# Attention and gated feed-forward on one core: side lists and sessions of score blocks, casting loads for chunks 1 and 2, and weights loaded behind chunk 0

## The chip, the cores and the metric

The kernel runs on one NeuronCore of a Trainium2 chip. The metric is the device time of one execution in microseconds, from the first to the last instruction. Five instruction streams run beside one another: TensorE (PE, with its weight loads as PEld), VectorE (DVE), ScalarE (ACT), GpSimd (POOL) and SyncE (SP); each works through its own instructions in the order in which they are written. Loads and stores are issued from the streams of SP, ACT and POOL; a load that also converts its type is issued from POOL.

## The reference

Four batches, eight heads, 768 positions, 64 numbers per head. Heads 0, 2 and 6 ("retrieval") see all earlier positions; the five others ("stream") see the first 4 positions and the last 64. The attention output, 3072 rows of 512, goes through two matrices with a gate between them.

```python
scores = scale * np.matmul(q, k.transpose(0, 1, 3, 2))
stream_keep = causal & (is_sink | in_win)              # n_sink = 4, window = 64
mask = np.where(retr, causal, stream_keep)             # by head
a = np.exp(np.where(mask, scores, -1e9) - max)
a = a / (np.sum(a, axis=-1, keepdims=True) + 1e-09)
x = np.matmul(a, v)                                    # then (3072, 512)
h = x @ w_in                                           # 512 -> 2048
g = h * (1.0 / (1.0 + np.exp(-beta * h)))
out = g @ w_out                                        # 2048 -> 512
```

All inputs and the output are float32; the kernel's matmuls take bfloat16.

## The kernel before

**Chunks.** The work is cut into 8 chunks, a batch and a half of the sequence each (384 positions, three tiles of 128). Before, the order alternates two batches: (0, first half), (1, first half), (0, second half), (1, second half), then the same for batches 2 and 3. A first half has 6 score blocks of 128x128 for a retrieval head and 5 for a stream head; a second half has 15 and 6.

**Stages of a chunk.** Keys and queries come in, are brought to bfloat16 and transposed, so that a pair of heads fills the 128 rows of KT and QT, 64 rows each. `attention(c, p)` (L561) works on one pair of heads: scores on TensorE (L603; the two heads sit on the two halves of the array's rows and run side by side), exponentials on ScalarE (L615), masks multiplied on VectorE (L630 to L648), the products with the values on TensorE (L663), whose 65th column gives the row sum, then the reciprocal and the scaling on VectorE (L667, L671). `x_transposed` (L674) transposes the result on TensorE (L683) or by DMA (L688). `first_part` (L695) multiplies by w_in: 16 groups of 4 matmuls (L701), each into a PSUM bank; ScalarE takes tanh of it (L703), VectorE combines both to the gate gT (L705) and frees the bank. `second_part` (L708) multiplies gT by w_out: three rows of 16 matmuls (L719) in steps of four, then the copy out of PSUM (L730, L732) and the store (L735).

**PSUM.** Eight banks: four for scores (`S_BANKS`), four for everything else (`G_BANKS`). A score group takes two rounds of banks for two heads, so up to four banks, and holds up to 384 columns in each; for the first two chunks it takes one round.

**Masks of the first chunks.** For chunks 0 and 1 the masks are added on TensorE: an identity matmul writes 0 or a large negative number into the bank ahead of the scores (L590).

**Loads.** For chunks 0, 1 and 2 keys and queries are loaded as float32 by SP and ACT, a pair of heads at a time (L379), cast on VectorE or ScalarE (L440) and transposed on TensorE (L448), three 128x128 pieces for each of k and q of a pair. From chunk 3 on POOL issues casting loads of rows (L417) and SP transposes them by DMA (L462). Values are loaded as float32 by SP (L392) and cast by POOL or VectorE (L497). The weights w_in and w_out come as four casting loads each from POOL (L399, L405); each is held back by a one-element copy (`held`, L365) until some earlier load has landed, by the table `W_AFTER`: w_in's first quarter behind the first values of chunk 0, the second behind chunk 1's last queries, the next two behind chunk 1's values, w_out behind w_in.

**What sets the order.** All streams are scheduled by hand, by a planner in the same file (class `Plan`): each step is a task with an engine, a cost, what it depends on and a priority; the planner runs through time, always gives the next free engine its best ready task, and the instructions are then written in that order. TensorE prefers attention; first and second products (`F1`, `F2`) fill up, by their running number and `F2_LAG`. The order is fixed when the program is built, and no engine changes it at run time. Where the plan shows TensorE idle before 36 us, matmuls on zeros are put in (`fill`, L811), and ten larger ones stand at the very start (`idle`, L338).

Of the kernel before, what the change touches and what calls it, by code (L numbers as in the profile page):

```python
# [16 lines left out]
class Slots:  # L17
# [18 lines left out]
    def take(self, n):  # L36
        order = sorted(range(len(self.free)), key=lambda i: (self.free[i], i))[:n]
        for i in order:
            self.free[i] = INF
        return order  # L40


class Hold:


    def __init__(self, slots, n=1):
        self.slots, self.n = slots, n
        slots.holds.append(self)
        self.got = None
        self.users = 0  # L50
        self.until = 0.0

    @property
    def buf(self):
        return self.slots.names[self.got[0]]

    @property
    def bufs(self):
        return [self.slots.names[i] for i in self.got]


class Task:
    __slots__ = ("name", "alts", "deps", "prio", "emit", "take", "drop", "mode", "land", "n_wait", "after",
                 "done", "start", "engine", "bias", "seq", "follow")

    def __init__(self, name, alts, deps, prio, emit, take=(), drop=(), mode=128, land=None, bias=0.0, follow=()):
        self.name, self.alts, self.prio, self.emit = name, alts, prio, emit
        self.deps = [d for d in deps if d is not None]
        self.take, self.drop, self.mode, self.land, self.bias = list(take), list(drop), mode, land, bias
# [5 lines left out]

class Plan:
# [3 lines left out]
    SWITCH = 100.0  # L80

    def __init__(self):
        self.tasks = []
        self.fill = None
# [7 lines left out]
    def run(self, pick):  # L92
        free = dict.fromkeys(self.SEM, 0.0)
        ready = {e: [] for e in self.SEM}
        for t in self.tasks:
            t.n_wait = len(t.deps) + len(t.follow)
            for d in t.deps + t.follow:
                d.after.append(t)

        def enter(t):  # L100
            for e, occ, lat in t.alts:
                at = max((d.start if e == d.engine == "PE" else d.done + self.SEM[e] for d in t.deps), default=0.0)
                at = max([at] + [d.start for d in t.follow])
                ready[e].append((at, t, occ, lat))
        for t in self.tasks:
            if not t.n_wait:
                enter(t)
        self.order = []
        self.mode = 128
        dma_free = 0.0  # L110
        lanes = {"hw": [], "sw": []}
        n = len(self.tasks)
        left = n
        while left:
            best = None
            for e, lst in ready.items():
                first = INF
                floor = free[e]
                cand = []
                for it in lst:  # L120
                    at = max(floor, it[0])
                    need = {}
                    for h in it[1].take:
                        if h.got is None:
                            need[h.slots] = need.get(h.slots, 0) + h.n
                            if not h.slots.turn(h):
                                at = INF
                    for slots, count in need.items():
                        at = max(at, slots.when(count))
                    if it[1].land is not None:  # L130
                        ln = lanes[it[1].land[0]]
                        if len(ln) >= 8:
                            at = max(at, ln[-8] + 60.0)
                    cand.append((at, it))
                    first = min(first, at)
                if first < INF and (best is None or first < best[0]):
                    best = (first, e, [c for c in cand if c[0] <= first])
            if best is None:
                self.stuck = [t for t in self.tasks if t.start is None]
                raise RuntimeError("the plan is stuck: " + ", ".join(t.name for l in ready.values() for _, t, _, _ in l[:4]))  # L140
# [3 lines left out]
            it = pick(e, now, [c[1] for c in cand])  # L144
            at, t, occ, lat = it
            for _, en in [(None, x[0]) for x in t.alts]:
                ready[en] = [x for x in ready[en] if x[1] is not t]
            if e == "PE":
                if t.mode != self.mode:
# [4 lines left out]
            if t.land is not None:  # L154
                kind, service = t.land
                begin = max(dma_free, now + occ + 1000.0)
                dma_free = begin + service
                t.done = dma_free + 1000.0
                lanes[kind].append(t.done)
            else:  # L160
                t.done = now + lat
            for h in t.take:
                if h.got is None:
                    h.got = h.slots.take(h.n)
            for h in t.drop:
                h.users -= 1
                h.until = max(h.until, t.done)
                if h.users == 0:
                    for i in h.got:
                        h.slots.free[i] = h.until + 55.0  # L170
            self.order.append(t)
            left -= 1
            for a in t.after:
                a.n_wait -= 1
                if a.n_wait == 0:
                    enter(a)
        self.end = max(t.done for t in self.tasks)
        return self.order

# [3 lines left out]
N_IDLE = 10  # L183
ROUNDS = 2
F2_LAG = 16.0
RAMP = 24000.0
RAMP_C = 2
FILL_END, FILL_SPARE = 36000.0, 120.0
N_F32 = 3
W_AFTER = [("v", 0, 0), ("q", 1, 3), ("v", 1, 0), ("v", 1, 2), ("wi", 1), ("wi", 2), ("wo", 0), ("wo", 1)]  # L190
C2_AFTER = ("wi", 2)
V2_AFTER = ("wi", 3)


def XT_PE(c, m):
    return c < 4 or (c == 7 and m % 2)
# [3 lines left out]
def kernel(  # L200
# [21 lines left out]
    stream = [h for h in range(H) if not retr[h]]  # L222
# [642 lines left out]
```

## Time and profile before

| what | value |
|---|---|
| median of 3 runs | 236.01 us (235.86 to 238.44) |
| span of the profiled execution | 236.1 us, which is also its time |
| instructions | 5174 |
| TensorE busy | 227.0 us, 96% |
| VectorE busy | 147.6 us, 63% |
| ScalarE busy | 157.3 us, 67% |
| GpSimd busy | 75.8 us, 32% |
| mean granted TensorE clock | 0.993 |
| read from HBM | 27.27 MB |

The page of the profile has the busy time of each engine, the span in 40 slices, the DMA queues, the chain of work that ended last, and the costliest groups of instructions. A group is named by its line in the kernel, engine and operation, with the tile written and the tiles read; behind the bar stand its busy time and the mean time of one, then the idle time of the engine just ahead of them and who ended it. Matmuls are pipelined: the time of one is longer than the distance from one to the next, so prices on TensorE are taken from start to start. The timeline gives start, length and instruction; what stands in brackets is the engine's idle time ahead of it and what ended that. Numbers like 64*128 are the rows and columns of the array in use.

### The profile page before, as it was taken

What the parts mean: (1) busy time and instruction counts of PE and PEld (TensorE: products, weight loads), DVE (VectorE), ACT (ScalarE), POOL (GpSimd) and SP (SyncE); (2) the same over time, 40 slices, a digit from 0 to 9 for tenths busy, and PEclk for the clock granted to TensorE, in tenths of its full rate; (3) what the DMA queues carried; (4) which work ended last, traced back from release to release, by engine and by line L of the source; (5) the groups of instructions that cost most, each with busy time, mean ns of one, the idle gap of its engine ahead of it and who ended that gap; (6) DMA issues with size and microseconds to landing.
All of it is one profiled execution on the core that took longest, in us unless ns stands there. A gap on an engine that the chain in (4) does not pass through costs nothing.

```text
span 236.1 us, 5174 instructions
## 1 busy us (share of the span) xinstructions
PE 227.0 (96%) x1898; PEld 125.8 (53%) x1898; DVE 147.6 (63%) x350; ACT 157.3 (67%) x339; POOL 75.8 (32%) x152
## 2 busy tenths in 40 slices
PE   7969989989999999999999999999999999999994
PEld 3546565544655545555554554555555555555553
DVE  5874878786857546558983886677756443434320
ACT  2947959797745569749786886889975645555400
POOL 4302431841991781799921334030000000000000
PEclk9997999999999999999999999999999999999999
DMA  6999999999899999999994696472121001111112
GB/s 199 247 212 230 174 172 261 254 176 100 158 168 186 158 199 152 122 193 229 130 174 105 148 131 117 109 149 61 21 78 47 24 22 46 47 44 44 44 47 89
DMA packets 93482, 31.10 MB, mean 132 GB/s; under 512 B 79744, under 2 KB 90512, under 8 KB 93456
## 3 DMA queue, kind: packets, MB, share of 16 engines
q1 hardware_dynamic: 56688, 22.10, 41.3%
q0 software_dynamic: 35904, 8.13, 41.0%
q10 hardware_dynamic: 864, 0.53, 0.7%
q8 instruction: 15, 0.25, 0.5%
q14 instruction: 11, 0.09, 0.1%
HBM read 27.27 MB, written 6.29 MB: 142 GB/s over the span
## 4 chain that ended last, share of the span: by engine, by line
PE 87%; DMA 5%; DVE 3%; SPq 2%; ACT 1%; issue 1%; ACTq 0%
PE bank L719 36%; PE bank L701 35%; PE bank L603 7%; PE bank L663 5%; DMA qs<-in_q_dram 5%; SPq L392 1%; PE bank L448 1%; PE bank L590 1%; PE bank L683 1%; SPq L379 1%; DVE gT L705 1%; DVE x L671 1%; ACT es L615 1%; ACT th L703 0%; DVE qkb L280 0%
## 5 line engine op out<-in xcount | busy, mean ns | idle before, releaser
L703 ACT ACTIVATE th<-bank,beta_h 128x384 f32<-128x384 f32 x128 | 74.4, 585 | 39.6 <-PE bank L701 31.7
L705 DVE SCALAR_TENSOR_TENSOR gT<-th,bank 128x384 bf16<-128x384 f32 x128 | 70.2, 551 | 46.8 <-ACT th L703 42.3
L701 PE MATMUL bank<-xT,w_in_sb 128*128 128x384 bf16 x512 | 95.9, 326 | 0.2 <-ACT xT L280 0.2
L719 PE MATMUL bank<-w_out_sb,gT 128*128 128x512 bf16 (+1 forms) x400 | 96.0, 371 | 0.0
L701 PEld LDWEIGHTS <-w_in_sb 128*128 128x128 bf16 x512 | 48.3, 98 | 37.2 <-issue 1.5
L719 PEld LDWEIGHTS <-gT 128*128 128x128 bf16 x400 | 37.0, 98 | 35.5 <-issue 2.6
L615 ACT ACTIVATE es<-bank 128x384 bf16<-128x384 f32 (+1 forms) x96 | 37.5, 477 | 11.6 <-PE bank L603 11.5
L615 ACT ACTIVATE esL<-bank 128x384 bf16<-128x384 f32 x68 | 28.0, 506 | 1.1 <-PE bank L603 1.0
L280 POOL COPY KO<-KT 128x128 bf16<-128x128 bf16 (+3 forms) x23 | 8.0, 370 | 48.5 <-DVE KO L280 17.8
L603 PE MATMUL bank<-QT,KT 64*128 64x128 bf16 (+2 forms) x258 | 22.9, 252 | 0.3 <-ACT QT L280 0.3
L417 POOL DMA_DIRECT2D qs<-in_q_dram x30 | 22.7, 786 | 0.9 <-issue 0.9
L417 POOL DMA_DIRECT2D ks<-in_k_dram x30 | 22.5, 797 | 0.0
L730 ACT ACTIVATE osb<-bank 128x512 f32<-128x512 f32 (+1 forms) x16 | 8.9, 559 | 13.3 <-DVE osb L732 9.9
L603 PEld LDWEIGHTS <-KT 64*128 64x128 bf16 x258 | 10.5, 95 | 13.3 <-issue 11.6
L671 DVE TENSOR_TENSOR x<-bank,rec 128x384 bf16<-128x384 f32 x32 | 17.3, 550 | 0.4
L630 DVE TENSOR_TENSOR es<-es,M 128x768 bf16<-128x768 bf16 (+1 forms) x24 | 12.5, 529 | 4.9 <-ACT es L615 4.9
L732 DVE TENSOR_SCALAR osb<-bank 128x512 f32<-128x512 f32 (+1 forms) x11 | 6.8, 617 | 10.3 <-PE bank L719 10.3
L667 DVE RECIPROCAL rec<-bank 128x6 f32<-128x6 f32 x32 | 6.0, 191 | 11.3 <-PE bank L663 11.2
L663 PEld LDWEIGHTS <-es 128*128 128x128 bf16 x268 | 10.6, 98 | 3.9 <-issue 0.7
L663 PE MATMUL bank<-VX,es 128*128 128x65 bf16 x200 | 11.6, 195 | 0.2 <-DVE gT L705 0.2
L280 POOL COPY VO<-VX 128x512 bf16<-128x512 bf16 (+2 forms) x7 | 6.0, 860 | 9.1 <-PE bank L603 5.3
L663 PEld LDWEIGHTS <-esL 128*128 128x128 bf16 x204 | 7.0, 97 | 1.1
(76 smaller groups left out, 149.9 us busy)
## 6 DMA issues: line engine op xcount, KB each, us to landing
vs<-in_v_dram SPq DMA_DIRECT2D x24, 256.0 KB, 5.4
out_dram<-osb SPq DMA_DIRECT2D x23, 256.0 KB, 2.2
ks<-in_k_dram SPq DMA_DIRECT2D x12, 192.0 KB, 5.9
w_in_sb<-in_moe_w_in_dram POOLq DMA_DIRECT2D x4, 512.0 KB, 8.0
w_out_sb<-in_moe_w_out_dram POOLq DMA_DIRECT2D x4, 512.0 KB, 9.0
qs<-in_q_dram SPq DMA_DIRECT2D x10, 192.0 KB, 8.6
ks<-in_k_dram POOLq DMA_DIRECT2D x30, 64.0 KB, 5.7
qs<-in_q_dram POOLq DMA_DIRECT2D x30, 64.0 KB, 4.3
```

Source lines behind the costliest of these rows:

```text
L280: (nc.scalar.copy if e == "ACT" else eng[e].tensor_copy)(out=out, in_=in_)
L417: ROW[name, c, t] = [dma(f"row{name}{c}.{t}.{a}", "POOL", 750, 850, list(deps), lambda e, t=t, a=a, r=r, i=i, src=src: e.dma_start(out=hol ...
L603: nc.tensor.matmul(to, kk(), of, start=not by_pe, stop=(r, at + n) == ends[a, r] or not by_pe)
L615: EX[a].append(P.add(f"exp{c}.{p}", [act(w * 128)], [t], prio, lambda _, a=a, place=place, w=w, bank=bank: nc.scalar.activation(out=es.buf ...
L630: masks.append(P.add(f"mask{c}.{p}", [dve(2 * (hi - lo) * 128, 0.53)], [EX[0][r], EX[1][r], t_mask], prio, lambda _, lo=lo, hi=hi: nc.vect ...
L663: nc.tensor.matmul(view()[:, i, a, 0:D + 1], es.buf[:, (base[a] + at) * 128:(base[a] + at + 1) * 128], val(), start=(j == 0), stop=(j == l ...
L671: nc.vector.tensor_mul(xo, view()[:, :, :, 0:D], rec.buf.to_broadcast([128, HT, 2, D]))
L701: nc.tensor.matmul(bank.buf[:, 0:HALF], w_in_sb[:, mo, fi * 128:(fi + 1) * 128], XTH[c].buf[:, mo, :], start=(mo == 0), stop=(mo == MO - 1))
L703: t = P.add(f"th{c}.{fi}", [act(HALF, 97)], [t, t_beta], c * 100, lambda _, fi=fi, bank=bank, th=th: nc.scalar.activation(out=th.buf, in_= ...
L705: GATE[c, fi] = P.add(f"gate{c}.{fi}", [dve(HALF)], [t], c * 100, lambda _, fi=fi, bank=bank, th=th: nc.vector.scalar_tensor_tensor(out=GH ...
L719: nc.tensor.matmul(bank.buf[:, 0:hi - lo], GH[c].buf[:, fi, ns * 128:(ns + 1) * 128], w_out_sb[:, fi, lo:hi], start=(fi == 0), stop=(fi == ...
L730: nc.scalar.activation(out=osb.buf[:, 0:h - l], in_=src, func=ACTF.Copy, scale=0.5)
```

## The change

The kernel is written anew in these points. The computation stays the same.

* **Chunk order and pairs.** Chunks now go batch by batch: (0, first half), (0, second half), (1, first half) and so on. In batch 0 heads are paired as neighbours, (0,1), (3,2), (4,5), (6,7); in the other batches as before, p with p + 4.
* **Side lists and sessions.** The score blocks of a chunk form two lists, one for the heads on each half of the array. From chunk 1 on, a session takes several banks for each side from these lists, up to four blocks (512 columns) in each, across heads. A first half is done in two sessions of 3 + 3 banks, a second half in three, with 4 + 3, 4 + 3 and 3 + 3; chunk 1 in four smaller ones. All exponentials of a chunk go into one large tile (`es_r`, two of them). Chunk 0 still goes pair by pair, and it alone adds its masks on TensorE; all others multiply them on VectorE, head by head.
* **Banks.** All eight banks are one pool.
* **Loads.** Of chunk 0, the first two pairs of k and q are loaded as float32 by SP and ACT and cast on the engines; the other half, and chunks 1 and 2 whole, come as casting loads of four heads from POOL, which need no cast. All values come as casting loads from POOL straight into VX. The weights follow in a fixed order on POOL's queue (`ORDER`): w_in's first two quarters behind chunk 0, then chunk 1's k and q, w_in's rest, chunk 1's values, w_out, chunk 2. The holding copies are gone. Chunks 3 to 7 keep row loads and DMA transposes.
* **Transposes.** Each head's 64 columns are transposed by themselves into one half of the bank's rows: six matmuls with 64 output rows for each of k and q of a pair, where three with 128 stood. x is transposed on TensorE for chunks 0 to 3 and all of chunk 7 (before: half of chunk 7).
* **Planner.** Loads are modelled as three queues that share the DMA engines (`Rings`). First and second products and the sessions from chunk 1 on stand in a written order (`P.script`, `STAGE_0`, `stage`), from which the planner may bring forward a task among the next eight. Fillers end at 16 us of the plan.

The core of the diff:

```diff
-N_F32 = 3
-W_AFTER = [("v", 0, 0), ("q", 1, 3), ("v", 1, 0), ("v", 1, 2), ("wi", 1), ("wi", 2), ("wo", 0), ("wo", 1)]
-FILL_END, FILL_SPARE = 36000.0, 120.0
+FILL_END, FILL_SPARE = 16000.0, 120.0
+STAGE_0 = [(3, 0, 0), (3, 0, 1), (3, 0, 2), (3, 0, 3), (4, 0, None)]
+SESSIONS = {0: [(3, 3), (3, 3)], 1: [(4, 3), (4, 3), (3, 3)]}
+SESSIONS_1 = [(3, 2), (3, 2), (3, 3), (2, 2)]
+ORDER = ["wi0", "wi1", "k1a", "q1a", "k1b", "q1b", "wi2", "wi3", "v10", "v11", "v12", "wo0", "wo1", "wo2", "wo3",
+         "k2a", "k2b", "q2a", "q2b", "v20", "v21", "v22"]
-    return c < 4 or (c == 7 and m % 2)
+    return c < 4 or c == 7
-    S_BANKS = Slots(banks[0:4])
-    G_BANKS = Slots(banks[4:8])
+    BANKS = Slots(banks)
-    esS = ring(4, [128, 14 * 128], BF16, "es")
-    esL = ring(2, [128, 32 * 128], BF16, "esL")
+    es_r = ring(2, [128, 75 * 128], BF16, "es")
+    def load_sw(c, h, name, prio):
+        to = Hold(qkb)
+        t = dma(f"ld{name}{c}.{h}", "POOL", 750, 768, 32, [], lambda e: e.dma_start(
+            out=to.buf.rearrange("p a t d -> p a (t d)"),
+            in_=rows_of(k if name == "k" else q, c)[h:h + 4].rearrange("a (p t) d -> p a (t d)", t=HT)), take=[to], prio=prio, follow=[t_m1])
...
+        LD["v", c, t] = dma(f"ldv{c}.{t}", "POOL", 1000, 256, 64, list(deps) + [t_ones[id(x)] for x in V_r.names], lambda e: e.dma_start(
+            out=VH[c].buf[:, t, :, 0:D], in_=rows_of(v, c)[:, t * 128:(t + 1) * 128, :].rearrange("h p d -> p h d")), take=[VH[c]], prio=prio, follow=follow)
...
-                for t in range(HT):
-                    nc.tensor.transpose(tp[:, t, :], hold.buf[:, i, t].rearrange("p a d -> p (a d)"), ident)
+                for t in range(HT):
+                    for a, (_, hold, i) in enumerate(src):
+                        nc.tensor.transpose(tp[half(a), t, :], hold.buf[:, i, t], ident)
...
+    def session(c, parts, prio, lane):
...
+        work = [(a, lo, SIDE[c, a][1][lo:lo + n], Hold(BANKS)) for a, lo, n in parts]
...
+            for _, a, h, kk, i, n, place, bank, ends in sorted(todo, key=lambda x: x[:2]):
+                nc.tensor.matmul(bank.buf[:, place * 128:(place + n) * 128], kk[1](), QH[c].buf[half(a), WHERE[c][h][1], i * 128:(i + n) * 128], start=not by_pe, stop=not by_pe or ends)
...
+            x = P.add(f"exp{c}.{a}.{lo}", [act(w * 128)], [t], prio, lambda _, e0=e0, w=w, bank=bank: nc.scalar.activation(
+                out=EH[c].buf[:, e0 * 128:(e0 + w) * 128], in_=bank.buf[:, 0:w * 128], func=ACTF.Exp, scale=scale), drop=[bank])
```

**POOL at the start** shows the loads' new order. First before, from the casts that hold the weights back (w_in_sb, w_out_sb: the weights; vs, qs: staged values and queries; KO: keys collected for stream heads; VO: values for them):

```order
L368 CAST w_in_sb<-vs_79 1x1
L399 DMA w_in_sb<-in_moe_w_in_dram 128x4x512
L280 COPY KO_87<-KT_83 128x128
L280 COPY KO_88<-KT_84 128x128 x2
L368 CAST w_in_sb<-qs_74 1x1
L399 DMA w_in_sb<-in_moe_w_in_dram 128x4x512
```

Then now, from the first load on:

```order
L490 DMA qkb_75<-in_k_dram 128x4x192
L490 DMA qkb_76<-in_q_dram 128x4x192
L497 DMA VX_97<-in_v_dram 128x8x64 x3
L502 DMA w_in_sb<-in_moe_w_in_dram 128x4x512 x2
L490 DMA qkb_77<-in_k_dram 128x4x192
L490 DMA qkb_78<-in_q_dram 128x4x192
L490 DMA qkb_79<-in_k_dram 128x4x192
L490 DMA qkb_80<-in_q_dram 128x4x192
L502 DMA w_in_sb<-in_moe_w_in_dram 128x4x512 x2
L385 COPY KO_93<-KT_89 128x128 x4
L497 DMA VX_98<-in_v_dram 128x8x64 x3
```

Two quarters of w_in now stand ahead of chunk 1's keys and queries, and nothing holds them back but their place.

**ScalarE in the middle of the program** shows what a visit to the scores leaves it to do (es, esL: exponentials; th: tanh of a first product). Before:

```order
L615 ACTIVATE esL_101<-bank_64 128x384
L615 ACTIVATE esL_101<-bank_65 128x384
L615 ACTIVATE esL_101<-bank_66 128x384
L615 ACTIVATE esL_101<-bank_63 128x384
L703 ACTIVATE th_113<-bank_68,beta_h 128x384
L615 ACTIVATE esL_101<-bank_64 128x384
L615 ACTIVATE esL_101<-bank_65 128x384
```

And now:

```order
L698 ACTIVATE es_104<-bank_70 128x512
L698 ACTIVATE es_104<-bank_67 128x512
L698 ACTIVATE es_104<-bank_65 128x512
L698 ACTIVATE es_104<-bank_68 128x512
L698 ACTIVATE es_104<-bank_66 128x512
L698 ACTIVATE es_104<-bank_69 128x512
L698 ACTIVATE es_104<-bank_64 128x512
L787 ACTIVATE th_114<-bank_70,beta_h 128x384
```

Four banks of 384 columns per visit have become seven of 512, and the first tanh behind them reuses the bank that the first of these exponentials read.

**TensorE's mode changes**, counted over its whole order: scores stand in 52 separate stretches before and in 25 now.

## Prediction before the change was run

> **What bounds the kernel now.** I read the head of the page first, then two long windows (columns after the stretch: its length, busy us of PE, PEld, DVE, ACT and POOL with their instruction counts, the granted clock, the DMA share and GB/s).
>
> ```profile
> span 236.1 us, 5174 instructions
> PE 227.0 (96%) x1898; PEld 125.8 (53%) x1898; DVE 147.6 (63%) x350; ACT 157.3 (67%) x339; POOL 75.8 (32%) x152
> PE 87%; DMA 5%; DVE 3%; SPq 2%; ACT 1%; issue 1%; ACTq 0%
> ...
> 0.00:34.00 34.00, 29.06 (x309) 17.37 (x310) 24.33 (x73) 22.66 (x56) 10.95 (x37) 0.95 1.00 206
> 34.00:236.00 202.00, 197.89 (x1591) 108.46 (x1589) 123.28 (x277) 134.65 (x284) 64.83 (x116) 1.00 0.81 119
> ```
>
> TensorE is the bound: 87% of the last-ended chain. The kernel has two parts. After 34 us PE is busy 197.9 of 202 us; 3.2 of the rest lie behind the last matmul, so that part ends sooner only if PE has less to do in it. Before 34 us the clock averages 0.95 and there are holes. So I ask two questions: when does PE become dense, and what is left for it then?
>
> In the PE timeline before is dense from 33.66 us on (start, length, instruction):
>
> ```profile
> 23.66 0.82 PE L701 MATMUL bank<-xT,w_in_sb 128*128 128x384 bf16 x4
> ...
> 33.66 7.96 PE L701 MATMUL bank<-xT,w_in_sb 128*128 128x384 bf16 x48
> ...
> 222.33 10.56 PE L719 MATMUL bank<-w_out_sb,gT 128*128 128x512 bf16 x64
> ```
>
> From 33.66 to the end it needs 236.1 − 33.7 = 202.4 us. The last product ends at 222.33 + 10.56 = 232.9, hence the 3.2 us tail, which the change leaves alone.
>
> **Prices of PE work**, from start to start in the dense part:
>
> ```profile
> 195.73 0.81 PE L701 MATMUL bank<-xT,w_in_sb 128*128 128x384 bf16 x4
> 196.38 1.03 PE L719 MATMUL bank<-w_out_sb,gT 128*128 128x512 bf16 x4
> 197.24 1.46 PE L701 MATMUL bank<-xT,w_in_sb 128*128 128x384 bf16 x8
> ...
> 97.56 0.51 PE L683 MATMUL bank<-idb,x 128*128 128x128 bf16 x6
> 97.90 1.89 PE L719 MATMUL bank<-w_out_sb,gT 128*128 128x512 bf16 x8
> ...
> 106.63 1.03 PE L719 MATMUL bank<-w_out_sb,gT 128*128 128x512 bf16 x4
> 107.59 0.34 PE L603 MATMUL bank<-QT,KT 64*128 64x128 bf16 x6
> 107.77 0.22 PE L603 MATMUL bank<-QT,KO 64*128 64x128 bf16 x2
> 107.82 0.22 PE L603 MATMUL bank<-QT,KT 64*128 64x128 bf16 x2
> 107.97 0.82 PE L701 MATMUL bank<-xT,w_in_sb 128*128 128x384 bf16 x4
> ...
> 62.39 2.00 PE bank L663 x63
> ```
>
> A first product (4 matmuls) takes 0.65 us, 162 ns each (1536 columns, so 2.36 columns per ns), a second product 0.86 us. A transpose takes 0.34/6 = 0.057, a product with values 2.00/63 = 0.032. Scores work on half the array, two heads side by side: the ten at 107.59 take 0.38 us, where 5 × 128 columns at 2.36 need 0.27; and the second product ahead of them takes 0.96 instead of 0.86. So **one visit to the half-height mode costs 0.11 + 0.10 = 0.21 us** beyond its columns.
>
> **Part 1, fewer visits.** In the order, scores stand in 52 visits before and 25 now. The columns are the same, since both sides of a session run side by side as pairs did. Of the visits behind the point of density 38 become 16: −22 × 0.21 = **−4.6 us** on the bound engine. The rest fall in the opening, which other engines set.
>
> **Part 2, the opening**, taken along the queues. What TensorE waits for there before is this (windows as above, then the ScalarE and PE rows):
>
> ```profile
> 16.00:17.00 1.00, 0.00 (x0) 0.00 (x0) 0.35 (x2) 0.00 (x0) 0.00 (x0) 1.00 1.09 163
> 17.00:18.00 1.00, 0.00 (x0) 0.00 (x0) 0.00 (x0) 0.57 (x2) 0.00 (x0) 1.00 1.08 281
> 19.00:20.00 1.00, 1.00 (x17) 0.76 (x14) 0.46 (x2) 0.51 (x1) 0.00 (x0) 0.50 1.16 287
> ...
> 17.43 0.51 ACT L280 CAST qkb<-qs 128x384 bf16<-128x384 f32 x1 [2.31 <-DMA qs<-in_q_dram]
> 17.84 0.65 ACT L615 ACTIVATE es<-bank 128x256 bf16<-128x256 f32 x2
> 18.27 0.41 PE L590 MATMUL bank<-Ac,idb 128*128 128x384 bf16 x1 [2.53 <-ACT es L615]
> ```
>
> A cast of chunk 1's queries stands in ScalarE's queue ahead of two exponentials of chunk 0; it waits for its load, PE idles 2.5 us, and then runs at half clock for 3.4 us. The change takes such casts off ScalarE: the loads cast. What it pays is that the loads of chunks 1 and 2, all values and the weights follow one another on POOL's queue. Rates for these (GB/s written; a casting load writes half of what it reads):
>
> ```profile
> 25.00:26.00 1.00, 1.00 (x13) 0.50 (x10) 0.88 (x3) 1.00 (x4) 0.70 (x2) 1.00 1.19 199
> 41.00:42.00 1.00, 1.00 (x7) 0.56 (x6) 0.91 (x2) 0.92 (x2) 0.00 (x0) 1.00 1.11 360
> 112.00:113.00 1.00, 1.00 (x15) 0.55 (x13) 0.93 (x3) 0.70 (x2) 1.00 (x5) 1.00 1.86 117
> ...
> q0 software_dynamic: 35904, 8.13, 41.0%
> w_in_sb<-in_moe_w_in_dram POOLq DMA_DIRECT2D x4, 512.0 KB, 8.0
> qs<-in_q_dram SPq DMA_DIRECT2D x10, 192.0 KB, 8.6
> ```
>
> At 25 us weights run alone at 199 GB/s: 512 KB, 2.6 us. At 41 us plain loads of keys and queries move 360 GB/s: a casting load of four heads reads 384 KB, at that rate 1.1 us; no row shows this form, so the ends are 1.1 and the weights' rate (192 KB written at 199, 1.0). At 112 us row loads cast pieces of 64 floats, as the values do, at 117 GB/s: 128 KB of values, 1.1 us. The other end is the page's mean software packet, 0.41 × 236.1 × 16 / 35904 = 43 ns: 64 packets per engine, if none overlap, 2.8 us. I take 1.1, since the window shows it directly, and keep 2.8 for a rival.
>
> From 2.2 us, then: the first half of chunk 0 lands by 4.4, its second half 6.6, values 9.8, two quarters of w_in 15.0, chunk 1's keys and queries 19.4, w_in's rest 24.6, chunk 1's values 27.9, w_out 38.3, chunk 2's keys and queries 42.7, each a microsecond later with its landing. Chunk 0's 16 exponentials leave x ready near 16, and the first product starts near 16.5 instead of 23.7, since its weights no longer wait behind chunk 1. Seven first products and chunk 1's transposes fill PE to about 23.5, and the first session ends a microsecond later. Then ScalarE decides: chunk 1's first three sessions fill 16 banks, there are 8, and the exponentials follow one another:
>
> ```profile
> L615 ACT ACTIVATE es<-bank 128x384 bf16<-128x384 f32 x76 | 31.7, 496 | 11.6 <-PE bank L603 11.5
> L615 ACT ACTIVATE es<-bank 128x256 bf16<-128x256 f32 x20 | 7.0, 407 | 0.0
> 125.50 1.53 ACT L615 ACTIVATE es<-bank 128x384 bf16<-128x384 f32 x4 [1.41 <-PE bank L603]
> ```
>
> In a row each 384-wide one adds (1.53 − 0.50)/3 = 0.34 to 0.38 us; 128 columns more cost 0.09, so a 512-wide one 0.45, no row showing one. From 24.5, 16 × 0.45 and a mask put chunk 1's values products, and with them density, at **32.5 us**. By then nine first products are done (before: five) and much of chunk 1, a large chunk where before had a small one.
>
> **The sum.** Against what before has left at 33.7 us, the order leaves at 32.5: 16 first-product matmuls fewer (−16 × 0.162 = −2.6); 43 values matmuls more (+43 × 0.032 = +1.4); 18 transposes of x more (+1.0), six of them because all of chunk 7 moves to TensorE; 14 blocks of scores fewer (−0.8); visits −4.6. Key transposes of chunk 2 become 48 with 64 output rows instead of 24 with 128. None stands in the trace. Ends: each two run side by side, as the score rows show for the other half-split (+0); or each costs 0.057 (+1.4); either with 3 visits at 0.21. I take the first with the visits, +0.6, the score rows being nearest.
>
> [...]
>
> Mask additions (32 matmuls to 16) and the idle-time fillers lie in the opening, where they hide under loads and exponentials; without that cover the additions gained would be 5504/2360 = 2.3 us. Wider exponentials and fewer casts relieve ScalarE and VectorE, which don't bind later. Total −5.0: 202.4 − 5.0 + 32.5 = 229.9, rounded to **230.0 us**, against 236.1 of the profiled execution, which is the median of the runs (236.01).
>
> **The rivals.**
> (a) *Half clock in the new hole.* From 24.5 to 32.5 PE has some 4.5 us of work in 8, and fillers now end at 16 us. Before, 2.5 us without work brought 3.4 us at 0.50. Two such spells cost 1.7 each, and half a microsecond where the order stalls for it: 234. Against it: the gaps are shorter, with matmuls between.
> (b) *The software queue starves the opening.* With values at 2.8 us instead of 1.1, chunk 1's keys come 5 us and its values 10 us late; the order is fixed, PE waits at those products, density moves to 42.5, and the time is 240, slower than before. It decides once chunk 1's values land over 6 us late, after about 35. Against it: the row loads of the window above, beside a busy VectorE.
>
> [...] Here six issues in a row took 4.5 us among VectorE work, 0.75 each, so the traces so far speak against a large effect.
>
> ```profile
> 112.59 4.49 POOL L417 DMA_DIRECT2D ks<-in_k_dram x6
> ```
>
> (c) *Sessions wait for banks.* In the dense part 15 sessions take 6 or 7 of all 8 banks at once. A bank of the first product comes back after tanh and gate, two rows of the groups (mean ns after the comma):
>
> ```profile
> L703 ACT ACTIVATE th<-bank,beta_h 128x384 f32<-128x384 f32 x128 | 74.4, 585 | 39.6 <-PE bank L701 31.7 <-DVE VX L280 1.9 <-ACT th L703 1.4
> L705 DVE SCALAR_TENSOR_TENSOR gT<-th,bank 128x384 bf16<-128x384 f32 x128 | 70.2, 551 | 46.8 <-ACT th L703 42.3
> ```
>
> That is 1.14 us, covered by the two second products (1.73) that mostly stand ahead. If ScalarE is one exponential behind, 0.45 × 15 = 6.8 us of stalls come back: 236.7. Against it: ScalarE is busy 135 of 202 us there and loses work.
>
> **How the numbers follow.** Forecast 0.60, (a) 0.16, (b) 0.14, (c) 0.10. A measurement of this kernel can tell about 1% (2.4 us, 233.6 to 238.4) from no change. Faster: 0.57 of the forecast, 0.05 of (a): 0.62. Same: 0.03, 0.11, 0.03 of (b), 0.07 of (c): 0.24. Slower: 0.11 of (b), 0.03 of (c): 0.14. The forecast's own range is 226 to 234: density at 29.5 with free transposes, or at 36. The whole range reaches from 225 to (b), 240.
>
> **What would show it.** Right: score visits 25, and the matmul ahead of each still 0.1 us longer; first products from about 16.5 us; density near 32.5, its start marked by values products; PE then busy but for about a microsecond. Part 2 is wrong if chunk 1's transposes start after 23 us, or if values loads land over 2 us apart. Part 1 is wrong if a session's surplus grows with its length. (a) shows as a second stretch at 0.50, (c) as waits of score weights for gate. The forecast falls if PE still has holes behind 36 us.

## The result and the profile after

| | before | after |
|---|---|---|
| median of 8 runs | 236.63 us (235.79 to 238.44) | 234.42 us (233.35 to 234.84) |
| span of the profiled execution | 236.1 us | 232.8 us |
| its own time | not given | 234.75 us |

The ratio is 0.9889, 95% interval 0.9858 to 0.9921: a gain of 1.1%, where the forecast said 230.0 us and 2.6%. The page's head:

```profile
span 232.8 us, 5227 instructions
PE 221.4 (95%) x1967; PEld 127.1 (55%) x1988; DVE 142.0 (61%) x353; ACT 151.9 (65%) x299; POOL 92.0 (40%) x141
```

TensorE's busy time fell by 5.6 us, the span by 3.3. About 1.4 of the 5.6 are not work: after's trace has 379 of the 400 second products (before's has all 400), and the profile counts 1.4 us of idle time in front of them. The rest, some 4.2 us, is still more than the span gained, so waiting came in. I look for it in the forecast's order: opening, visits, dense part.

**The opening** in the PE timeline of after (start, length, instruction, and in brackets the idle time ahead with what ended it):

```profile
17.36 2.11 PE L784 MATMUL bank<-xT,w_in_sb 128*128 128x384 bf16 x12
19.40 0.53 PE L542 MATMUL bank<-idb,qkb 128*64 128x128 bf16 x12
...
23.69 0.53 PE L542 MATMUL bank<-idb,qkb 128*64 128x128 bf16 x12
...
27.80 0.27 PE L689 MATMUL bank<-QT,KT 64*128 64x256 bf16 x1 [1.25 <-ACT es L698]
...
30.57 0.28 PE L742 MATMUL bank<-VX,es 128*128 128x65 bf16 x4
...
33.83 0.19 PE L742 MATMUL bank<-VO,es 128*128 128x65 bf16 x1 [0.52 <-DVE gT L789]
```

First products start at 17.4 (forecast 16.5), chunk 1's key transposes run from 19.4 to 24.1, the sessions then wait for exponentials, and the values products stand from 30.6 to 34.2, around the 32.5 of the forecast. From 34.19 us to 54.5 PE works without a gap of 0.1 us.

**The visits.** A session in the dense part, and the second products on both sides of it:

```profile
108.93 1.89 PE L804 MATMUL bank<-w_out_sb,gT 128*128 128x512 bf16 x8
110.75 0.62 PE L689 MATMUL bank<-QT,KT 64*128 64x128 bf16 x12
...
111.41 1.25 PE L804 MATMUL bank<-w_out_sb,gT 128*128 128x512 bf16 x4
```

Eight second-product matmuls at 0.216 need 1.73 us and take 1.82 from start to start; ten blocks on the longer side need 10 x 128 / 2360 = 0.54 and take 0.66. That is 0.09 ahead and 0.12 inside: the price of 0.21 again, for a session of six banks. From 71 to 190 us all 13 sessions show it, the stretches between them are longer than their own prices by 1.27 us in all, and that is the 0.10 of each visit. There is no waiting left in that part.

**The dense part** holds what went wrong, in chunk 2. The PE timeline of after, then the page of waits by line:

```profile
54.72 0.23 PE L689 MATMUL bank<-QT,KO 64*128 64x128 bf16 x2 [0.18 <-DVE osb L818]
54.77 0.32 PE L689 MATMUL bank<-QT,KT 64*128 64x128 bf16 x4
55.03 2.12 PE L784 MATMUL bank<-xT,w_in_sb 128*128 128x384 bf16 x12
56.99 0.19 PE L742 MATMUL bank<-VX,es 128*128 128x65 bf16 x1
57.43 0.42 PE L742 MATMUL bank<-VX,es 128*128 128x65 bf16 x8 [0.25 <-DVE es L722]
...
58.18 0.19 PE L742 MATMUL bank<-VX,es 128*128 128x65 bf16 x1
60.45 0.51 PE L764 MATMUL bank<-idb,x 128*128 128x128 bf16 x6 [2.08 <-DVE x L752]
60.89 0.78 PE L689 MATMUL bank<-QT,KT 64*128 64x128 bf16 x12
...
62.22 1.49 PE L804 MATMUL bank<-w_out_sb,gT 128*128 128x512 bf16 x3 [0.33 <-issue]
63.49 2.75 PE L784 MATMUL bank<-xT,w_in_sb 128*128 128x384 bf16 x12
```

```profile
PE bank L764 <- DVE x L752: 2.1, 1, 2.1
PE bank L689 <- ACT es L698: 1.5, 2, 1.3
```

PE works off the values products of chunk 2's first pairs and then stands before the transposes of x, for which VectorE has still to mask, gate and scale. The hole of 2.08 us is the largest wait of the run; the 1.5 us of the second row are the opening's. The twelve first-product matmuls at 63.49 show what follows: 2.75 us where those at 55.03 took 2.12. The windows of after (length; busy us of PE, PEld, DVE, ACT, POOL; clock; DMA share; GB/s):

```profile
59.00:60.00 1.00, 0.00 (x0) 0.00 (x0) 1.00 (x4) 0.00 (x0) 1.00 (x2) 1.00 1.64 178
...
61.00:62.00 1.00, 0.88 (x16) 0.69 (x15) 0.97 (x3) 1.00 (x3) 1.00 (x3) 0.68 2.20 171
62.00:63.00 1.00, 0.79 (x2) 0.30 (x2) 0.49 (x1) 1.00 (x3) 1.00 (x2) 0.50 2.34 161
63.00:64.00 1.00, 1.00 (x4) 0.46 (x3) 0.26 (x1) 0.89 (x3) 1.00 (x2) 0.50 1.80 111
```

The clock is at 0.50 from 61.36 to 64.77 us. (The 0.33 us ahead of the three second products at 62.22 is no wait: the trace holds only three of the four there.) At the prices of the rest of the run the work from the session at 53.87 us to the values products at 66.08 needs 7.3 us; it took 12.2. These 4.9 us are more than the whole difference to the forecast.

**Why PE had nothing else to do** can be read in the code. Chunk 0's second products, and only these, go quarter by quarter over three row blocks (`F2[c] = [by_quarter[ns, 0][i] for i in range(4) for ns in range(HT)]`), so that up to three banks hold unfinished sums. Chunk 2's two sessions take six banks each at once. At the first, three and six would be nine of eight: it must wait for a row block to end (the tenth of twelve steps). At the second, behind the hole, two row blocks are still open, and two and six are all eight: every other bank must be free first, those of the first products, of the values products and of the transposes too. No first or second product that needs a new bank may pass a session that waits for banks; and the two steps that would end the open row blocks are the tenth and eleventh from the second session on in the written order, while the planner sees the session and eight more. What was left were chunk 2's transposes of x.

### The profile page after: what moved, and what is told of

It reads as the page before. It is cut to its first block, busy times and chain, and to the rows that moved or that the text cites. A ratio compares the mean times of both kernels' runs of the same rounds, so it can differ in the third digit from the quotient of the medians.

```text
span 232.8 us, 5227 instructions
## 1 busy us (share of the span) xinstructions
PE 221.4 (95%) x1967; PEld 127.1 (55%) x1988; DVE 142.0 (61%) x353; ACT 151.9 (65%) x299; POOL 92.0 (40%) x141
## 4 chain that ended last, share of the span: by engine, by line
PE 90%; ACT 4%; DVE 3%; issue 1%
PE bank L804 36%; PE bank L784 35%; PE bank L689 6%; PE bank L742 5%; ACT es L698 4%; PE bank L542 2%; PE bank L764 2%; PE bank L448 2%; PE bank L674 1%; PE bank L968 1%; DVE gT L789 1%; DVE es L722 1%; DVE x L752 0%; PE bank L692 0%; DVE KO L385 0%
## 5 line engine op out<-in xcount | busy, mean ns | idle before, releaser
L804 PE MATMUL bank<-w_out_sb,gT 128*128 128x512 bf16 (+1 forms) x379 | 89.0, 372 | 1.4 <-issue 0.3
L698 ACT ACTIVATE es<-bank 128x512 bf16<-128x512 f32 (+3 forms) x132 | 61.3, 585 | 16.3 <-PE bank L689 16.3
L722 DVE TENSOR_TENSOR es<-es,M 128x768 bf16<-128x768 bf16 (+1 forms) x35 | 18.3, 527 | 18.4 <-ACT es L698 18.0
L497 POOL DMA_DIRECT2D VX<-in_v_dram x24 | 21.4, 915 | 8.2 <-DMA w_out_sb<-in_moe_w_out_dram 4.9
L519 POOL DMA_DIRECT2D kr<-in_k_dram x30 | 22.6, 795 | 3.6 <-DMA w_out_sb<-in_moe_w_out_dram 1.7
L519 POOL DMA_DIRECT2D qr<-in_q_dram x30 | 22.3, 762 | 1.6 <-DMA kr<-in_k_dram 0.8
L689 PE MATMUL bank<-QT,KT 64*128 64x128 bf16 (+2 forms) x281 | 19.8, 241 | 1.8 <-ACT es L698 1.5
L742 PEld LDWEIGHTS <-es 128*128 128x128 bf16 x472 | 17.6, 97 | 5.0 <-issue 0.9
L742 PE MATMUL bank<-VX,es 128*128 128x65 bf16 x392 | 18.8, 193 | 0.3 <-DVE es L722 0.3
L718 DVE TENSOR_TENSOR es<-es,Mc 128x384 bf16<-128x384 bf16 x21 | 7.4, 352 | 5.5 <-ACT es L698 5.5
L742 PE MATMUL bank<-VO,es 128*128 128x65 bf16 x80 | 9.9, 193 | 0.6 <-DVE gT L789 0.5
```

Of the source, the lines that this page charges most:

```text
L497: LD["v", c, t] = dma(f"ldv{c}.{t}", "POOL", 1000, 256, 64, list(deps) + [t_ones[id(x)] for x in V_r.names], lambda e: e.dma_start(out=VH[ ...
L519: ROW[name, c, t] = [dma(f"row{name}{c}.{t}.{a}", "POOL", 750, 256, 32, [], lambda e, t=t, a=a, r=r, i=i, src=src: e.dma_start(out=hold.bu ...
L689: nc.tensor.matmul(bank.buf[:, place * 128:(place + n) * 128], kk[1](), QH[c].buf[half(a), WHERE[c][h][1], i * 128:(i + n) * 128], start=n ...
L698: x = P.add(f"exp{c}.{a}.{lo}", [act(w * 128)], [t], prio, lambda _, e0=e0, w=w, bank=bank: nc.scalar.activation(out=EH[c].buf[:, e0 * 128 ...
L722: made[h] = [P.add(f"mask{c}.{h}", [dve(n * 128, 0.53)], list({EXPS[c, at + i] for i in range(n)}) + [t_mask], prio, lambda _, n=n, m0=m0, ...
L742: nc.tensor.matmul(view()[:, i, a, 0:D + 1], EH[c].buf[:, e0 * 128:(e0 + 1) * 128], val(), start=(j == 0), stop=(j == len(mine) - 1))
```

## Experiments

The theory (A): this jam of banks, by its hole and the half clock behind it, took the missing gain. The rivals: VectorE is late with x whatever the order (B); the larger sessions lose time throughout, by visits or banks (C); the slow stretch has another cause than the hole (D). All spans are of one profiled execution, the ratios are to runs of the kernel before in the same set; the medians of these lie between 236.6 and 237.4 us, so ratios of different sets can differ by 0.3% for that alone.

### rows: chunk 0's second products row block by row block

```diff
-        if c == 0:
-            F2[c] = [by_quarter[ns, 0][i] for i in range(4) for ns in range(HT)]
-        else:
-            F2[c] = [t for key in sorted(by_quarter) for t in by_quarter[key]]
+        F2[c] = [t for key in sorted(by_quarter) for t in by_quarter[key]]
```

> The changed kernel with one edit: chunk 0's second products are taken row block by row block, as in all other chunks, instead of quarter by quarter over three row blocks, so that one bank holds a half-finished row block instead of three. Theory A (the missing gain is the hole of PE before chunk 2's transposes of x, 58.2 to 60.4 us, and the half clock behind it, because six banks for chunk 2's second session were not to be had while unfinished row blocks held two): hole and 0.50 stretch go, 2.8 + 1.7 us and some tenths of small waits; span 232.8 - 4.6 = 228.2, time about 230.2. Rival B (VectorE is late with x of chunk 2, whatever the order): another wait of 1 to 2 us appears at the transposes of x or at the next session, span 231 or more. Rival C (the gain went into the larger sessions, by their visits or by waits for banks throughout): span within 0.5 us of 232.8.

Measured: span 228.3 us, time 229.87 (229.65 to 229.99), ratio 0.9687 (0.9672 to 0.9703). The PE timeline of rows at the same place of the program:

```profile
53.73 0.19 PE L742 MATMUL bank<-VX,es 128*128 128x65 bf16 x1
53.98 1.67 PE L804 MATMUL bank<-w_out_sb,gT 128*128 128x512 bf16 x7
55.58 0.61 PE L689 MATMUL bank<-QT,KT 64*128 64x128 bf16 x12
...
56.24 0.51 PE L764 MATMUL bank<-idb,x 128*128 128x128 bf16 x6
```

Second products and the session stand between the values products and the transposes of x; behind the opening no wait of more than a quarter of a microsecond is left. Theory A gave 228.2; B and C fall here. The quarter order was of no use by then: no wait for w_out's last quarter shows in rows.

### four: smaller sessions in chunk 2 alone

```diff
-            for n0, n1 in (SESSIONS_1 if c == 1 else SESSIONS[h2]):
+            for n0, n1 in (SESSIONS_1 if c == 1 else [(2, 2)] * 3 if c == 2 else SESSIONS[h2]):
```

> The changed kernel with one edit: chunk 2's scores in three sessions of four banks instead of two of six; chunk 0's second products stay quarter by quarter, so that up to three banks hold unfinished row blocks. Theory A (the hole comes from six banks asked for at once while unfinished row blocks hold two or three of eight): the hole and its half clock go as they did in rows, for one more visit at 0.2 us; span 228.5, at most 229.5. Rival H (unfinished row blocks do it by themselves, through the order of second products, whatever the session's size): a hole of 1 us or more stays before 62 us, span 230.5 or more.

Measured: span 228.3, time 230.29 (230.00 to 230.41), ratio 0.9718 (0.9665 to 0.9770). The PE timeline of four:

```profile
57.45 1.03 PE L804 MATMUL bank<-w_out_sb,gT 128*128 128x512 bf16 x4
58.31 0.50 PE L764 MATMUL bank<-idb,x 128*128 128x128 bf16 x6
58.65 1.03 PE L804 MATMUL bank<-w_out_sb,gT 128*128 128x512 bf16 x4
59.60 0.39 PE L689 MATMUL bank<-QT,KT 64*128 64x128 bf16 x5
```

The unfinished row blocks are back, the session asks for four banks instead of six, and the hole is gone just the same. So neither the quarter order nor the six banks make the hole alone; their sum does.

### ahead: the planner sees two steps more

```diff
-AHEAD = 8
+AHEAD = 10
```

> The changed kernel with the planner's look-ahead at 10 steps instead of 8; nothing else. The planner then puts chunk 0's last two second products (0.86 us each, their data ready since about 50 us) ahead of chunk 2's values products, where the changed kernel's PE waits, and chunk 2's transposes of x behind its second session. Theory A: no hole of 2 us, no 0.50 stretch unless a wait of over 1 us is left ahead of the session; span 229.5 to 231. Theory A says that rows does better, since the session still needs six banks: a wait of 0.5 to 1 us ahead of it stays here and not in rows. Rival B: a wait of the same 2 us moves to the second session, span 232 or more.

Measured: span 230.7, time 232.72 (232.29 to 233.27), ratio 0.9810 (0.9788 to 0.9831). The PE timeline of ahead:

```profile
58.63 1.03 PE L804 MATMUL bank<-w_out_sb,gT 128*128 128x512 bf16 x4
59.59 0.46 PE L689 MATMUL bank<-QT,KT 64*128 64x128 bf16 x8
60.34 0.34 PE L689 MATMUL bank<-QT,KT 64*128 64x256 bf16 x4 [0.29 <-ACT osb L816]
```

The withheld second products fill the hole, the clock stays at 1.00 there, and what is left is the jam itself: the session waits in its midst for a bank that ScalarE frees by copying out a row block (osb). It takes 1.14 us where it takes 0.66 in rows, the session ahead of it 1.16 for 0.77 and the one behind it 1.60 for 0.98; a first product waits 0.7 us for x of a later chunk. That is most of the 2.4 us by which ahead stays behind rows: the hole was filled, the jam not cured.

### fill: zeros in the hole

```diff
-        if n < 1 or until > FILL_END or not free:
+        if n < 1 or (until > FILL_END and not 57000.0 < since < until < 60500.0) or not free:
```

> The changed kernel with 19 multiplications of zeros (256 columns, some 0.11 us each, results unused) put where PE waits for x of chunk 2 (58.2 to 60.4 us); the order of everything else is the same. Theory A says that the half clock of 61.4 to 64.8 us follows from the hole: it goes, PE is busy in the hole but no earlier through it, span 232.8 - 1.7 = 231.1. Rival D (the slow stretch comes from something else than missing work, for example the dense stretch ahead): the 0.50 stretch stays, span 232.8, and the hole is busy with zeros.

Measured: span 231.5, time 233.63 (232.53 to 233.81), ratio 0.9836 (0.9803 to 0.9869). The PE timeline of fill, then one of its windows:

```profile
58.49 2.24 PE L968 MATMUL bank<-zeros 128*128 128x256 bf16 x19
60.73 0.51 PE L764 MATMUL bank<-idb,x 128*128 128x128 bf16 x6
```

```profile
63.00:64.00 1.00, 1.00 (x9) 0.60 (x7) 0.95 (x3) 1.00 (x5) 0.99 (x2) 1.00 2.26 143
```

PE gets to the transposes no earlier relative to the values products (3.46 us behind the first of them, as in after), but the clock stays at 1.00 behind them. The hole was the cause of the half clock (D falls), and the clock alone cost 1.3 us of span. fill came to this place 0.28 us later than after, with a half-clock stretch in its opening (28.7 to 32.1 us) that after has not, so 1.6 is nearer; the medians of the spans of all runs of the two differ by 1.2. The other 3 us are waiting.

### single: the visit price, 36 times more

```diff
-SESSIONS = {0: [(3, 3), (3, 3)], 1: [(4, 3), (4, 3), (3, 3)]}
+SESSIONS = {0: [(1, 1)] * 6, 1: [(1, 1)] * 9 + [(1, 0)] * 2}
```

> The kernel of rows, with chunk 2 and later in sessions of one bank a side: 51 visits to the half-height mode behind 36 us instead of 15, the same score columns. Theory A with the prediction's price of 0.21 us a visit: 36 x 0.21 = 7.6 us more than rows, span about 235.8. Rival C (the large sessions lose time by waiting for 6 or 7 banks, so small ones give some back): less than 4 us more than rows, and in rows the matmul groups ahead of a session are longer than 0.10 us over their own price.

Measured: span 235.9, time 237.62 (237.07 to 238.34), ratio 1.0012 (0.9990 to 1.0034). Against rows 7.6 us of span, 36 x 0.21 = 7.6. Small sessions give nothing back, so with the jam gone the large ones of this kernel wait for no banks. And with sessions of one bank a side the new kernel is no faster than the one before.

### keys: chunk 1's keys ahead of w_in's second quarter (on rows)

```diff
-ORDER = ["wi0", "wi1", "k1a", "q1a", "k1b", "q1b", "wi2", ...
+ORDER = ["wi0", "k1a", "q1a", "k1b", "q1b", "wi1", "wi2", ...
```

> The kernel of rows with one edit in the order of loads on the software queue: chunk 1's keys and queries stand behind the first quarter of w_in, ahead of the second (instead of behind both). Theory A (ScalarE's exponentials set the point from which PE is dense, so what starts them earlier moves it): chunk 1's first session starts near 20 us instead of 24, the exponentials then run among the tanhs of chunk 0, density 1 to 2 us earlier, span 226.3 to 227.3 against 228.3. Rival E (the second quarter of w_in, now later, holds up the first products): density as late as before or later, span 228 or more.

Measured: span 226.2, time 228.11 (227.91 to 228.26), ratio 0.9645 (0.9608 to 0.9682). The PE timeline of keys:

```profile
19.74 0.27 PE L689 MATMUL bank<-QT,KT 64*128 64x128 bf16 x2
...
32.70 0.81 PE L784 MATMUL bank<-xT,w_in_sb 128*128 128x384 bf16 x4
```

The first session starts at 19.7 us instead of 23.5 in rows (24.1 in after); the first products behind the last values products of the opening start at 32.70, in rows at 34.39. The span follows, a little more than foreseen. Some of the 2.1 us is not the order's: the profiled execution of rows has a half-clock stretch in its opening and that of keys none. The two runs of rows with a mean clock of 1.00 have spans of 227.9 and 228.1, against 226.2 to 226.5 for keys, so 1.4 to 1.9 us come from the order.

### twice: more exponentials in the opening (on rows)

```diff
-            x = P.add(f"exp{c}.{a}.{lo}", [act(w * 128)], [t], prio, lambda _, e0=e0, w=w, bank=bank: nc.scalar.activation(...
+            x = P.add(f"exp{c}.{a}.{lo}", [act(w * 128)], [t], prio, lambda _, e0=e0, w=w, bank=bank, n=2 if c == 1 and lo % 8 == 0 else 1: [nc.scalar.activation(... for _ in range(n)]
```

> The kernel of rows, in which 11 of chunk 1's 20 exponentials are issued twice in a row (same input, same output), 9 of them among the 16 ahead of the values products that end the opening; the order is else unchanged. Theory A (ScalarE decides in the opening, 0.5 us an exponential of 512 columns): density 9 to 11 x 0.5 = 4.5 to 5.5 us later, span about 233, with PE and the loads waiting longer. Rival F (loads of values or weights decide, ScalarE has slack): less than 1.5 us more.

Measured: span 234.1, time 235.78 (235.49 to 236.29), ratio 0.9973 (0.9952 to 0.9994). The windows of twice, a row of its PE timeline, then the row of exponentials on ScalarE, first in rows and then in twice:

```profile
28.00:32.00 4.00, 1.66 (x20) 1.07 (x18) 1.09 (x2) 3.91 (x9) 1.82 (x3) 0.50 1.26 207
...
36.00:40.00 4.00, 1.89 (x40) 1.45 (x41) 1.90 (x5) 3.94 (x9) 1.62 (x2) 1.00 1.48 194
```

```profile
40.03 0.81 PE L784 MATMUL bank<-xT,w_in_sb 128*128 128x384 bf16 x4
```

```profile
24.08 7.95 ACT L698 ACTIVATE es<-bank 128x512 bf16<-128x512 f32 x16
...
24.89 13.60 ACT L698 ACTIVATE es<-bank 128x512 bf16<-128x512 f32 x25
```

ScalarE is busy 3.9 of 4 us while PE is idle more than half. The point from which PE is dense moved from 34.39 to 40.03, by 5.6 us (4.8 if counted from the first session, which starts 0.8 us later here). Rival F, under 1.5 us, falls: ScalarE sets this point, as the forecast had it. Only nine of the eleven repeats stand ahead of it; the other two come at 40.6 and 41.7 us. The nine lengthen ScalarE's row from 7.95 to 13.60 us, 0.63 each. That is no price for an exponential in a row: 0.63 is the mean length of one of 512 columns in after, so it fits a repeat that starts only when its twin has ended, while in rows the sixteen start 0.48 us apart (the forecast took 0.45).

### both and x3: x transposed by DMA (on keys)

```diff
 def XT_PE(c, m):
-    return c < 4 or c == 7
+    return c < 2          # both
+    return c < 3          # x3
```

> The kernel of keys, with x of chunks 2, 3 and 7 transposed by DMA instead of on TensorE: 36 transposes less, 36 x 0.057 = 2.0 us of PE. If PE alone decides in the dense part: span 2.0 us below keys, about 224.7. Rival: the transposes by DMA come late for chunk 2 or 7, PE shows a new wait of a microsecond or more ahead of that chunk's first products, span 226 or more.

> The kernel of keys with x of chunks 3 and 7 alone transposed by DMA (chunk 2 stays on TensorE): 24 transposes less, 24 x 0.057 = 1.4 us of PE. If PE alone decides there: span 226.2 - 1.4 = 224.8, time about 226.6. Rival: the transposes by DMA hold up chunk 7's first products or, as with chunk 2's in both, the transposes of queries on the same queue: a PE wait of 0.5 us or more, span 225.5 or more.

Measured: both 227.42 us (226.34 to 230.75), ratio 0.9596 (0.9544 to 0.9648), and its profiled execution was the slowest of five (230.75); x3 227.76 (227.49 to 228.07), ratio 0.9613 (0.9569 to 0.9657), span 226.0. x3 cannot be told from keys (0.9608 to 0.9682). The four other runs of both (226.34 to 227.80) all lie below those of keys (227.91 to 228.26), the medians by 1.05 us, and two of them, with spans of 224.6 and 225.0, are at the 224.7 of the forecast. One row of the PE timeline of both, then two of x3:

```profile
67.37 0.27 PE L689 MATMUL bank<-QT,KT 64*128 64x256 bf16 x1 [2.04 <-DMA QT<-qr]
```

```profile
91.98 0.23 PE L689 MATMUL bank<-QT,KO 64*128 64x128 bf16 x2 [0.94 <-DVE gT L789]
...
92.66 2.75 PE L804 MATMUL bank<-w_out_sb,gT 128*128 128x512 bf16 x12 [0.30 <-DVE gT L789]
```

In x3 the 24 transposes should save 1.4 us, but PE waits 1.24 us for gates: 0.94 in the midst of a session, for a bank that a gate frees, and 0.30 ahead of the second products behind it. The forecast of 224.8 was wrong by just this wait. It is the sign that rival (c) of the first forecast had named. In keys six transposes of x stand among the first products ahead of that session; that the missing cover makes the wait is likely, not tested. In both a session waits 2.04 us for queries whose transposing DMA is late (the rival had looked for the wait at the first products), and half clock follows from 68.4 us on; x3, with chunk 2's x back on TensorE, has no such wait. The profile of both is of its longest execution alone, so how often this wait comes is open.

### again: the kernel before, for its own time

> The kernel before, unchanged, for the time of a profiled run beside its own span. Theory G (a run's time holds about 1.8 us more than its span, as in rows, 229.99 against 228.3, and after, 234.75 against 232.8): the profiled run has a span of 234 to 236.1 and a time 1.5 to 2.2 above it, so the forecast, which set the span of 236.1 against a median of 236.0, left that out. Rival: time and span agree within 0.5 us for this kernel.

Measured: span 235.3, time of that execution 237.16, median 237.17 (235.78 to 238.42). The time is 1.9 us above the span; it is 1.7 in rows, twice and keys, 1.9 in four and 1.95 in after.

## Why the prediction was off, point by point

* **The step that failed** is the one behind rival (c). It asked whether a first product's bank comes back in time (1.14 us, covered by 1.73 of second products) and answered for the 15 sessions alike. For the dense part that holds: no session from 71 us on waits. It did not count the banks that are held by something else, and in chunk 2 these were unfinished row blocks: three at the first session, two at the second, beside the six that each session asks for. So "PE then busy but for about a microsecond" failed in one place, by 4.9 us, 4.5 of which rows got back by one line. Rival (c) had the right resource and the wrong place and price (15 small waits of 0.45).
* **Rival (a)** put the half clock into the opening. In after it came behind chunk 2's hole instead. In rows the opening does have such a stretch:

```profile
29.00:30.00 1.00, 1.00 (x5) 0.53 (x4) 0.96 (x2) 1.00 (x4) 0.88 (x2) 0.54 1.25 212
30.00:31.00 1.00, 1.00 (x8) 0.51 (x6) 1.00 (x3) 1.00 (x4) 0.60 (x1) 0.50 1.23 206
```

  ScalarE is busy 1.00 of each us there. Density came at 34.39 instead of 34.19 although the first session started 0.6 us earlier, so the stretch cost about 0.8 us, not the 1.7 of the forecast; between whole runs of rows with it (mean clock 0.99) and without (1.00) the spans differ by 0.3. There, with ScalarE as the bound, half clock cost less than its price.
* **Part 1** was right: 0.21 us a visit, also for large sessions, tested by 36 more (7.6 of 7.6).
* **Part 2** was right in its mechanism. First products were 0.9 us late and an exponential took 0.48 instead of 0.45 us; all the same the 54 products with values, three transposes and eight score matmuls that the forecast put behind 32.5 us (2.3 us of work) were done at 34.19, as if PE had been dense from 31.9. Rival (b) fell: PE shows no wait for a load in the opening, and chunk 1's values landed 0.83 us apart (27.5 to 29.2 us in after). The microsecond that the forecast added to each load for its landing was an estimate, and no run shows it by itself; with it, chunk 1's last queries were due at 20.4 us and landed at 21.5, its last values at 28.9 (29.2), w_out at 39.3 (39.3).
* **The sum** of the dense part was too small a gain. Rows needs 228.3 - 34.4 = 193.9 us where before needs 202.4: -8.5, where the forecast had -5.0 and the 2.3 just named, -7.3. The rest, 1.2 us, fits waits that stood in before's 202.4 and that I took for work; no run tests that. In before's PE timeline, chunk 2's transposes wait for the copies out of the banks:

```profile
47.87 0.27 PE L603 MATMUL bank<-QT,KT 64*128 64x256 bf16 x1 [0.31 <-ACT QT L280]
...
49.62 0.33 PE L448 MATMUL bank<-idb,qkb 128*128 128x128 bf16 x3 [0.25 <-DVE QT L280]
```

  The 24 transposes there took 2.4 us from start to start, 1.4 by their price. The key transposes with 64 rows took 0.03 each and 1.7 us in all, so that pairs ran in parallel, as taken.
* **Span and time.** The forecast set before's span of 236.1 equal to its median of 236.0 and gave a span as its time; the table of the kernel before does the same. A profiled execution's time is 1.7 to 2.0 us above its span, so the metric holds more than the way from the first to the last instruction. So the profiled execution of before must have taken about 238 us, and 229.9 of span meant about 231.6 of time. Of the 4.4 us by which the forecast of the time was off, 2.9 are span and the rest is this. In spans the account closes: 229.9 + 4.9 (hole and clock) - 1.2 (waits of before) - 0.6 (opening) = 233.0, measured 232.8; the time adds 1.6 to 2.0.

The median of before lies at 236.0 in one set of runs and at 237.4 in another. The granted clock goes with it: of 49 executions of before with a clock on record, 20 with a mean of 0.998 to 1.000 took 235.9 us (median), 24 with 0.991 to 0.993 took 237.3, and 5 with 0.986 took 238.8. One stretch of 3.41 us at 0.50 lowers the mean over 235 us by 0.007, so the three groups fit none, one and two such stretches. In both profiles of before (0.993 and 0.992) there is one, in the opening, at 18.4 and 19.8 us. What stays open is where the others have theirs, and why some have none.

## What to carry to other kernels

Before letting a group of matmuls take many banks at once, count what holds banks at that moment for another reason, above all sums left open to run several rows side by side: here two or three open row blocks and a group of six asked for all eight banks or for nine, and one line was worth 4.5 us, more than the 2.2 us by which the medians of the whole rewrite differ. A planner that finds nothing to place shows the hole in its own plan; read its idle list and ask which ready work it was not allowed to see. And compare spans with spans: a time contained 1.7 to 2.0 us outside them here.

## What the runs showed of the hardware

* Half clock came in stretches of 3.41 us. After had one (61.36 to 64.77 us) behind a wait of 2.08 us. In rows a wait of 1.26 us stands ahead of the stretch in the opening (29.08 to 32.50 us by its windows); in after the same wait of 1.25 us did not bring one. Ahead of the last matmul the clock records of before (18.41 to 21.82 us) and after have one slow stretch of 3.41 us each; twice's windows add up to 6.9 us, about two of them; keys and x3, with means of 0.997, have none, since one would take 0.007 off the mean. The full-clock stretches ahead of the slow ones are whole multiples of 3.41 us (13.65 us = 4 times in before, 54.61 = 16 times in after). Counted back in steps of 3.41 us from the slow stretch, the wait of rows lies whole within one step, that of after across the border of two (windows of rows, then of after):

```profile
25.67:29.08 3.41, 1.86 (x26) 1.16 (x24) 1.49 (x4) 3.41 (x8) 1.53 (x3) 1.00 1.84 181
...
23.81:27.22 3.41, 2.40 (x42) 1.62 (x41) 1.59 (x4) 3.37 (x8) 1.61 (x6) 1.00 2.02 170
27.22:30.64 3.42, 2.55 (x30) 1.63 (x30) 2.41 (x5) 3.42 (x9) 2.93 (x4) 1.00 1.34 204
```

  PE is busy for 1.86 us of the step in rows, behind which the clock fell, and for 2.40 and 2.55 us of the two in after, behind which it did not. In the steps right ahead of the slow stretches of before and after it is busy for 0.82 and 1.33 us. So in these profiles where a wait lies seems to matter as well as its length. No run moved one on purpose, and the limit is open.
* Exponentials of 512 columns followed one another every 0.48 us here: the 16 of the opening in rows (24.08 to 31.72 us) and in after (24.69 to 32.34, the start of the tanh behind them), and in after a row of six in the dense part (3.04 us, the last one's 0.64 included).
